# Key-bit rows inside the third score product of two periods, a new order of the first eight periods, and halved last products

## The chip, the cores and the metric

One core of one Trainium2 chip runs the whole program. The metric is the device time of one execution in microseconds (us). Engines are named as in the profile: PE (TensorE matmul), PEld (its weight load), DVE (VectorE), ACT (ScalarE), POOL (GpSimd), SP (SyncE, which issues all transfers here; its queue is SPq).

## What is computed

Bucketed attention over 2 batches, 8 heads, 768 positions and 64 channels, then two channel-mixing blocks. Only the attention concerns the change:

```python
q_bits = (np.einsum('bhsd,dk->bhsk', q, proj) > 0)      # 6 bits, a bucket number
k_bits = (np.einsum('bhsd,dk->bhsk', k, proj) > 0)
mask = q_bucket[:, :, :, None] == k_bucket[:, :, None, :]
scores = np.where(mask, scale * np.matmul(q, k.transpose(0, 1, 3, 2)), -1e9)
attn = exp(scores - max) / (sum + 1e-09)
x = attn @ v                      # then x = moe(x), x = moe2(x): 512 channels, 2048 hidden
```

moe2 ends in `x + relu(xn @ w_ch1) @ w_ch2`; its rows are the output of the kernel.

## The kernel before

Every product is made at reduced precision from a high and a low part (`hi`, `lo`), so one score tile is high x high, high x low and low x high. The equality of buckets is added to the scores by seven more rows of the contraction: six bits as large plus or minus values and one constant, so that a differing bucket sinks the score.

The attention runs in 48 periods (`NPER`) of two query tiles of 128 rows each. A head has three periods. A period p and tile i has: `S` or `D` (scores on PE, 128 x 772), `M` (row maximum, DVE), `E` (exponential, ACT), `R2` (reciprocal, DVE), `n` (normalising, POOL), `U` (12 transposes in three groups of four, PE), `H` and `L` (high and low part of the transposed weights, ACT and DVE), `PV` (12 products of 256 columns, PE), `O` and `X` (evacuation, ACT and DVE).

For heads 1 to 15 the operands are stacked by six transfers per head (`stack_dma`, lines 241 to 254; word `sk` in the order): `tq` x `tk` has 128 rows (high and low of q against high of k twice), `tq2` x `tk2` has 71 rows (high q against low k on rows 0 to 63, the bits on rows 64 to 70, put there by the two transfers of `stk_bits`, word `sb`). So a tile is four matmuls (`s_mm`, line 326). For head 0, the first three periods, nothing is stacked yet: `direct_mm` (line 497, word `D`) makes three products of two matmuls from the split tiles, with K = 64 rows in period 0 and K = 128 in periods 1 and 2, where `kz` is a copy of k with zeros in the lower 64 rows. `direct_bits` (line 512, word `Q`) then adds the bits by two matmuls of 7 rows.

What comes before the scores: `load0` and `raw_load` (`lr`) fetch q and k, `sh`/`sl` split them into high and low, `pb` splits the projection, `ac` (line 273) multiplies k and q by it for pair 0 (two matmuls for each half of k and q, x = 0, 1 for k and 2, 3 for q), `ay`, `ab`, `aw` turn the sign into bits on ACT, DVE and DVE or POOL; `bc`, `by`, `bb`, `bw` do this for pairs 1 to 3. `fk` writes two padding columns from the constants `cst_sb`.

Nothing schedules itself: each engine executes its instructions in the order in which the text `head` (line 684) names the steps, then the periodic `plan`, then the texts `tail`, `half1`, `trans`, and the rounds of the last block. One word is one step; a last number usually picks the engine (0: ACT or DVE, 1: POOL). All transfers go through SP's queue in the same order, and a transfer that waits for its data holds up those named behind it.

`warm(n)` (line 491) makes n transposes of the identity whose result nobody reads: 16 at the start, 17 in `head` between the bits of period 0 and `D.1.0`. At the end, `o_mm` (line 1172) makes the six matmuls of 512 columns of an output tile, `o_add` (line 1182) adds the residual and sends 128 rows of 2 KB out. The last round runs this for t = 0 to 5.

Of the kernel before, what the change touches and what calls it, by code (L numbers as in the profile page):

```python
# [9 lines left out]
F32 = mybir.dt.float32  # L10
F32R = mybir.dt.float32r
# [22 lines left out]
def attn_moe_kernel(  # L34
# [36 lines left out]
    def bank(tag, name):
        return psum.tile([128, 512], F32, tag=tag, name=name)
# [10 lines left out]
    M = const.tile([128, 4, 2, 2], F32, name="M")  # L83
# [181 lines left out]
    bits_t = {}  # L265
# [167 lines left out]
    def theta_steps(c, x, y):  # L433
# [19 lines left out]
    plan = (  # L453
# [15 lines left out]
    bk0 = wide(ap_, 64, "pn1", "bk0", 2)  # L469
# [20 lines left out]
    def warm(n):  # L490
        ps = bank("T0", "warm")
        for x in range(n):
            pe.transpose(ps[:, 0:128], ident, ident)  # L493

    def direct_mm(p, i):

        ps = psum.tile([128, 2, 512], F32, tag=f"S{i}", name=f"s{p}_{i}")
        s_ps[p, i] = ps
        r = slice((2 * p + i) * 128, (2 * p + i + 1) * 128)
        K, kk = (64, [hl["k", 0, y] for y in (0, 1)]) if p == 0 else (128, kz)  # L500
        for x, y in ((0, 0), (0, 1), (1, 0)):
            for hf in range(2):
                pe.matmul(  # L503
                    ps[:, hf, 0:HW], hl["q", 0, x][0:K, r],
                    kk[y][0:K, hf, :], start=(x + y == 0), stop=False,
                )

    def bits_q(r):
        hf, x = divmod(r.start, HALF)
        return bits_t[0][0:7, hf, x:x + 128]  # L510
# [72 lines left out]
    for i in range(8):  # L583
        c, x = divmod(i, 2)
# [74 lines left out]
    def bp_(x, e):  # L659
# [22 lines left out]
    )

    head = """
        sh.k.0.0.0 pb.0.0 pb.0.2 sl.k.0.0.0 pb.0.1 sh.k.0.1.0 sl.k.0.1.0 sh.q.0.0.0 sl.q.0.0.0 sh.q.0.1.0 ac.0
        sl.q.0.1.0 fk ac.1 ay.0 ay.1 kz.1.1 ac.2 ay.2 D.0.0 ab.0 lr.3.0 ab.1 ac.3 sh.k.1.2.0 D.0.1 ay.3 ab.2
        sh.q.1.2.0 aw.0.1 aw.1.1 pb.1.0 aw.2.0 kz.0.0 ab.3 Q.0.0 M.0.0 Q.0.1 warm.17 pb.1.2 E.0.0 lr.3.1 M.0.1
        sl.q.1.2.1 E.0.1 pb.1.1 D.1.0 sl.k.1.2.0 sh.k.3.2.0 Q.1.0 tb.0 lr.2.0 R2.0 lr.2.1 aw.3.0 M.1.0 n.0.1
        sk.1 sh.k.2.2.0 D.1.1 n.0.0 E.1.0 U.0.2 Q.1.1 U.0.0 sh.q.3.2.0 sl.k.2.2.0 sl.k.3.2.0 U.0.1 sl.q.3.2.1
        H.0.0 D.2.0 M.1.1 H.0.2 bc.0.1 L.0.2 L.0.0 Q.2.0 sh.q.2.2.0 E.1.1 M.2.0 by.0 tb.1 H.0.1 bc.1.0 D.2.1  # L690
        lv.0 bb.0 sl.q.2.2.1 L.0.1 by.1 sb.1 R2.1 Q.2.1 bw.0.1 n.1.0 E.2.0 bb.1 vh.0.0 lr.4.0 bc.3.1 M.2.1
        vh.0.1 S.3.0 lr.5.0 vl.0.0.0 bc.2.0 by.3 bw.1.1 E.2.1 U.1.0 by.2 M.3.0 S.3.1 bb.3 n.1.1 U.1.1 E.3.0
        vl.0.1.1 R2.2 bb.2 U.1.2 tb.2 bw.3.1 H.1.0 M.3.1 n.2.0 H.1.1 S.4.0 PV.0 H.1.2 E.3.1 L.1.0 L.1.1 lr.4.1
        M.4.0 tb.3 R2.3 sh.k.4.0.0 gl U.2.0 n.2.1 O.0 n.3.0 bw.2.1 L.1.2 X.0 S.4.1 sl.k.4.0.1 U.2.1 E.4.0 U.2.2
        H.2.0 M.4.1 H.2.1 sk.2 H.2.2 E.4.1 S.5.0 lv.1 sh.q.4.0.0 PV.1 lr.5.1 L.2.0 sb.2 L.2.1 M.5.0 L.2.2 R2.4
        O.1 tb.4 X.1 n.3.1 sh.k.4.1.1 E.5.0 U.3.0 S.5.1 U.3.2 U.3.1 n.4.1 H.3.0 H.3.2 H.3.1 S.6.0 M.5.1 sk.4
        n.4.0 L.3.0 vh.1.0 L.3.2 PV.2 E.5.1 L.3.1 sl.q.4.0.1 U.4.2 O.2 vh.1.1 M.6.0 sk.3 R2.5 X.2 vl.1.0.1
        U.4.0 sb.3 S.6.1 tb.5 H.4.0 sl.k.4.1.0 sb.4 U.4.1 H.4.2 M.6.1 n.5.0 E.6.0 H.4.1 L.4.0 E.6.1 PV.3 n.5.1
        S.7.0 U.5.0 sh.q.4.1.0 O.3 L.4.2 L.4.1 M.7.0 H.5.0 U.5.2 S.7.1 X.3 R2.6 tb.6 U.5.1 E.7.0 H.5.1 H.5.2
        M.7.1 PV.4 vl.1.1.1 L.5.0 sl.q.4.1.1 n.6.0 E.7.1 tb.7 O.4 L.5.1  # L700
    """

    for w in head.split():
# [284 lines left out]
    W1, W2 = {}, {}  # L988
# [135 lines left out]
    h_t, ps_t, sn_t, c_t, o_t = {}, {}, {}, {}, {}  # L1124
# [295 lines left out]
    zctx.close()  # L1420

# [49 lines left out]
```

## Time and profile before

| | us |
|---|---|
| three runs of the kernel before | 664.65, 665.45, 670.51 |
| their median | 665.45 |
| the profiled execution | 665.16 |
| its span, first to last instruction | 663.4 |
| PE busy in the span | 657.4 (99%) |
| DVE, ACT, POOL busy | 556.9, 416.7, 310.4 |

The profile is one execution. The span is 1.76 us shorter than the time of the same execution, which also holds what lies around it. Busy times of PE are modelled from pipelined matmuls; the distance between the starts of two matmuls of one row says what one costs in a stream. The chain of work is the path followed back from the last instruction; its pieces have a start, a length and a count.

### The profile page before, as it was taken

To read this page: it belongs to the slowest core of one execution; us is meant where nothing else is said; L and a number is where in the kernel's file an instruction comes from. 1 tells how busy PE (TensorE), PEld (TensorE's weight loads), DVE (VectorE), ACT (ScalarE), POOL (GpSimd) and SP (SyncE) were. 2 spreads that over 40 slices of the span, in tenths; PEclk is the share of its full clock that TensorE was granted. 3 is DMA by queue.
4 is the path that set the end of the run, shared out by engine and by line. 5 is a ranking of instruction groups with operands and counts; after the bars stand their busy time and mean duration, and the time that the engine had idled before them with its cause. 6 is when DMAs were issued, how large, how long until landed. Compare 5 with 4: busy or idle time off the path is not lost.

```text
span 663.4 us, 11202 instructions
## 1 busy us (share of the span) xinstructions
PE 657.4 (99%) x3769; PEld 591.7 (89%) x3769; DVE 556.9 (84%) x999; ACT 416.7 (63%) x864; POOL 310.4 (47%) x419
## 2 busy tenths in 40 slices
PE   9999999999999999999999999999999999999997
PEld 7999999999999888888888888989998999999996
DVE  6999998999999999999888889986767686867654
ACT  6899998999999886776435534553333433333321
POOL 5887887667787644233433133434150505051400
PEclk9999999999999999999999999999999999999999
DMA  8977544575530411222422122101112121311022
GB/s 247 241 172 171 142 106 114 126 165 124 132 91 1 160 54 57 81 77 98 144 81 64 48 96 68 60 1 64 64 65 75 53 96 34 105 53 33 0 80 111
DMA packets 32230, 62.24 MB, mean 94 GB/s; under 512 B 4466, under 2 KB 11460, under 8 KB 32173
## 3 DMA queue, kind: packets, MB, share of 16 engines
q1 hardware_dynamic: 32173, 61.53, 32.6%
q8 instruction: 30, 0.49, 0.3%
q14 instruction: 27, 0.22, 0.1%
HBM read 39.98 MB, written 3.15 MB: 65 GB/s over the span
## 4 chain that ended last, share of the span: by engine, by line
PE 96%; DVE 2%; DMA 1%; issue 0%; ACT 0%; SPq 0%; POOL 0%; POOLq 0%
PE o L1180 20%; PE acc L853 15%; PE o L405 10%; PE s L332 10%; PE t L380 9%; PE Z L1145 8%; PE a L895 5%; PE v L1145 5%; PE th L787 3%; PE zy L1145 2%; PE Y L1145 2%; PE bits L286 2%; PE s L503 1%; PE warm L493 1%; PE ut L880 1%; PE xt L964 1%
## 5 line engine op out<-in xcount | busy, mean ns | idle before, releaser
L1180 PE MATMUL o<-arena,hh 128*128 128x512 f32 x384 | 118.9, 391 | 0.0
L367 POOL TENSOR_SCALAR pn<-p,l,M 128x768 f32<-128x768 f32 x96 | 94.7, 986 | 38.6 <-DVE l L363 25.8
L340 DVE TENSOR_REDUCE M<-s 128x1 f32<-128x772 f32 x96 | 91.0, 949 | 3.6 <-PE s L515 2.2
L101 DVE TENSOR_TENSOR ptl<-t,pth 128x512 fp32r<-128x512 f32 x144 | 90.6, 680 | 1.5 <-ACT pth L389 1.3
L356 ACT ACTIVATE p<-s,M 128x772 f32<-128x772 f32 x96 | 87.6, 912 | 2.7 <-DVE M L340 2.2
L117 POOL TENSOR_SCALAR cs<-st 128x512 f32<-128x512 f32 (+2 forms) x68 | 44.7, 663 | 84.1 <-DVE cy L131 75.1
L1180 PEld LDWEIGHTS o<-arena,hh 128*128 128x128 f32 x384 | 71.5, 188 | 13.7
L389 ACT ACTIVATE pth<-t 128x512 fp32r<-128x512 f32 x144 | 81.1, 599 | 3.9 <-PE t L380 2.5
L332 PE MATMUL s<-tk,tq 128*128 128x386 f32 (+1 forms) x360 | 82.8, 351 | 0.0
L380 PE MATMUL t<-ident,pn 128*128 128x128 f32 x576 | 80.1, 273 | 0.0
L853 PE MATMUL acc<-arena,tokh 128*128 128x512 f32 x240 | 75.3, 395 | 0.0
L1180 PE MATMUL o<-arena,hl 128*128 128x512 f32 x192 | 75.2, 392 | 0.0
L380 PEld LDWEIGHTS t<-ident,pn 128*128 128x128 f32 x576 | 68.5, 141 | 5.7 <-POOL pn L367 0.6
L1153 ACT ACTIVATE sn<-Z 128x384 f32<-128x384 f32 x39 | 19.2, 492 | 67.2 <-PE Z L1145 67.2
L332 PEld LDWEIGHTS s<-tk,tq 128*128 128x128 f32 (+1 forms) x360 | 59.4, 190 | 0.1
L853 PEld LDWEIGHTS acc<-arena,tokh 128*128 128x128 f32 x240 | 44.0, 188 | 8.5
L1187 DVE TENSOR_TENSOR U<-o,U 128x512 f32<-128x512 f32 x48 | 32.9, 689 | 21.3 <-PE o L1180 20.5
L853 PE MATMUL acc<-arena,tokl 128*128 128x512 f32 x120 | 46.9, 391 | 0.0
L405 PE MATMUL o<-pth,vv 128*128 128x256 f32 x288 | 45.9, 295 | 0.1
L114 ACT ACTIVATE cy<-st 128x512 f32<-128x512 f32 (+2 forms) x72 | 39.6, 562 | 8.1 <-DVE tokl L101 2.5
L131 DVE SCALAR_TENSOR_TENSOR cy<-cy,cs 128x512 uint32<-128x512 uint32 (+2 forms) x72 | 41.4, 575 | 3.6
L125 DVE SCALAR_TENSOR_TENSOR cs<-st,cs 128x512 uint32<-128x512 uint32 (+2 forms) x76 | 44.0, 579 | 0.2
(257 smaller groups left out, 1482.8 us busy)
## 6 DMA issues: line engine op xcount, KB each, us to landing
st<-in_w_dram SPq DMA_DIRECT2D x36, 256.0 KB
st<-in_w_dram SPq DMA_DIRECT2D x14, 512.0 KB
tk<-hik SPq DMA_DIRECT2D x30, 193.0 KB
tq<-hiq SPq DMA_DIRECT2D x30, 192.0 KB
st<-in_wrT_dram SPq DMA_DIRECT2D x12, 384.0 KB
st<-in_wiT_dram SPq DMA_DIRECT2D x12, 384.0 KB
vs<-in_v_dram SPq DMA_DIRECT2D x8, 384.0 KB
tk<-lok SPq DMA_DIRECT2D x15, 193.0 KB
```

The costliest lines, as they stand in the source:

```text
L101: eng.tensor_tensor(out=o, in0=i, in1=f(hi), op=ALU.subtract)
L117: eng.tensor_scalar(out=s, in0=f(t)[:, :, 1], scalar1=0.0, scalar2=1.0, op0=ALU.mult, op1=ALU.mult)
L332: pe.matmul(ps[:, hf, 0:HW], lt[0:K, x * 128:(x + 1) * 128], rt[0:K, hf, :], start=(K == 128), stop=(K != 128),)
L340: vec.tensor_reduce(out=m_t[p][:, 0, i:i + 1], in_=s_ps[p, i][:, :, 0:HW], axis=AX.XY, op=ALU.max, negate=True)
L356: act.activation(pt, ps[:, :, 0:HW], AF.Exp, bias=m[:, 0, i:i + 1], accum_out=l_t[p][:, 0, i:i + 1])
L367: pool.tensor_scalar(out=pn.rearrange("p (h c) s -> p h (c s)", h=2), in0=p_t.pop((p, i))[:, :, 0:HALF], scalar1=l_t[p][:, 1, i:i + 1], sc ...
L380: pe.transpose(ps[:, w * 128:(w + 1) * 128], pn_t[p, i][:, c, :], ident)
L389: act.activation(ph, t_ps[p, u], AF.Copy)
L405: pe.matmul(ps, vv[:, c, e].rearrange("p a d -> p (a d)"), x[:, c::NI, :], start=(k == 0), stop=(k == 2 * NI - 1),)
L853: pe.matmul(acc, w[:, x, t * 128:(t + 1) * 128], z[:, x, y, :], start=(j == 0 and k == 0), stop=(j == NI - 1 and k == 5),)
L1145: pe.matmul(ps_t[r, b], W1[g][y][:, w, d, :], XB[s][x][:, z, d, :], start=(first == 1 and k == 0), stop=(k == 5), skip_group_check=True,)
L1180: pe.matmul(ps, lt[:, i * 128:(i + 1) * 128], W2[g][:, y, x, :], start=(k == 0), stop=(k == 5))
```

## The change

In periods 1 and 2 the third direct product becomes high q against low k over 71 rows: `tq2_0` (one more use of the ring `tq2`) takes high q by one transfer (`stack_q`, word `sq0`), and two transfers (`stack_b`, word `sb0`) put the bits of k on rows 64 to 70 of `kz[1]` and those of q on rows 64 to 70 of `tq2_0`. The steps `Q.1.0`, `Q.1.1`, `Q.2.0`, `Q.2.1` are gone; period 0 keeps its `Q`. The 16 transposes at the start become 38 products of a zeroed 128 x 128 part of `pb_lo` with itself, zeroed by DVE; the 17 later ones become 36. The order of the first eight periods is new. The last output tile is made in two halves of 256 columns in two banks, each added and sent by itself.

```diff
+    tq2_0 = bp.tile([128, S], F32R, tag="tq2", bufs=3, name="tq2z")
...
-        K, kk = (64, [hl["k", 0, y] for y in (0, 1)]) if p == 0 else (128, kz)
-        for x, y in ((0, 0), (0, 1), (1, 0)):
+        qh, ql = (hl["q", 0, y] for y in (0, 1))
+        kh, kl = [hl["k", 0, y] for y in (0, 1)] if p == 0 else kz
+        terms = ((qh, kh, 128), (ql, kh, 128), (tq2_0, kl, 71))
+        if p not in (1, 2):
+            K = 64 if p == 0 else 128
+            terms = ((qh, kh, K), (qh, kl, K), (ql, kh, K))
+        for x, (lt, rt, K) in enumerate(terms):
             for hf in range(2):
                 pe.matmul(
-                    ps[:, hf, 0:HW], hl["q", 0, x][0:K, r],
-                    kk[y][0:K, hf, :], start=(x + y == 0), stop=False,
+                    ps[:, hf, 0:HW], lt[0:K, r], rt[0:K, hf, :],
+                    start=(x == 0), stop=(x == 2 and p in (1, 2)),
                 )
+
+    def stack_q():
+        sp.dma_start(out=f(tq2_0[0:64]), in_=f(hl["q", 0, 0][0:64]))
+
+    def stack_b():
+        sp.dma_start(out=f(kz[1][64:71]), in_=f(bk0[0:7]))
+        sp.dma_start(out=f(halves(tq2_0[64:71])), in_=f(halves(bits_t[0][0:7])))
...
     sp.dma_start(out=pbr[:, 1:NP], in_=pb[:, 1:NP])
+    vec.memset(f(pb_lo[:, 1]), 0.0)
+    ps = bank("T0", "warm")[:, 0:128]
+    for x in range(38):
+        pe.matmul(ps, pb_lo[:, 1], pb_lo[:, 1], start=True, stop=True)
+    for n in (0, 2, 3):
+        vec.memset(f(pb_lo[:, n]), 0.0)
     make_identity(nc, ident)
     pool.memset(halfpi, math.pi / 2)
-    pool.memset(f(pb_lo), 0.0)
     for t in kz:
         pool.memset(f(t[64:128]), 0.0)
-    warm(16)
...
     head = """
-        sh.k.0.0.0 pb.0.0 pb.0.2 sl.k.0.0.0 pb.0.1 sh.k.0.1.0 sl.k.0.1.0 sh.q.0.0.0 sl.q.0.0.0 sh.q.0.1.0 ac.0
-        sl.q.0.1.0 fk ac.1 ay.0 ay.1 kz.1.1 ac.2 ay.2 D.0.0 ab.0 lr.3.0 ab.1 ac.3 sh.k.1.2.0 D.0.1 ay.3 ab.2
-        sh.q.1.2.0 aw.0.1 aw.1.1 pb.1.0 aw.2.0 kz.0.0 ab.3 Q.0.0 M.0.0 Q.0.1 warm.17 pb.1.2 E.0.0 lr.3.1 M.0.1
-        sl.q.1.2.1 E.0.1 pb.1.1 D.1.0 sl.k.1.2.0 sh.k.3.2.0 Q.1.0 tb.0 lr.2.0 R2.0 lr.2.1 aw.3.0 M.1.0 n.0.1
-        sk.1 sh.k.2.2.0 D.1.1 n.0.0 E.1.0 U.0.2 Q.1.1 U.0.0 sh.q.3.2.0 sl.k.2.2.0 sl.k.3.2.0 U.0.1 sl.q.3.2.1
-        H.0.0 D.2.0 M.1.1 H.0.2 bc.0.1 L.0.2 L.0.0 Q.2.0 sh.q.2.2.0 E.1.1 M.2.0 by.0 tb.1 H.0.1 bc.1.0 D.2.1
-        lv.0 bb.0 sl.q.2.2.1 L.0.1 by.1 sb.1 R2.1 Q.2.1 bw.0.1 n.1.0 E.2.0 bb.1 vh.0.0 lr.4.0 bc.3.1 M.2.1
...
+        sh.k.0.0.0 pb.0.0 sl.k.0.0.0 pb.0.2 pb.0.1 ac.0 sh.k.0.1.0 sh.q.0.0.0 sl.k.0.1.0 ac.1 sl.q.0.0.0
+        sh.q.0.1.0 sl.q.0.1.0 ay.0 ay.1 ac.2 ay.2 ac.3 fk ab.0 D.0.0 D.0.1 aw.0.1 ay.3 ab.1 aw.1.1 sq0 ab.2
+        aw.2.0 pb.1.0 pb.1.1 Q.0.0 Q.0.1 warm.36 ab.3 sh.k.1.2.0 lr.3.0 kz.1.1 aw.3.1 kz.0.1 M.0.0 lr.2.0 sb0
+        sh.q.1.2.0 M.0.1 lr.2.1 E.0.0 sl.q.1.2.0 sh.k.3.2.0 D.1.0 sl.k.1.2.0 sl.k.3.2.0 E.0.1 tb.0 sh.k.2.2.0
+        lr.3.1 pb.1.2 sk.1 sh.q.2.2.0 R2.0 sl.k.2.2.0 n.0.0 D.1.1 bc.0.1 sh.q.3.2.0 bc.1.0 U.0.0 lv.0 M.1.0
+        E.1.0 n.0.1 by.0 M.1.1 D.2.0 by.1 sl.q.2.2.0 bb.0 E.1.1 sb.1 tb.1 sl.q.3.2.1 U.0.1 bb.1 bw.0.1 H.0.0
+        H.0.1 U.0.2 H.0.2 M.2.0 L.0.0 D.2.1 E.2.0 vh.0.0 bc.2.1 lr.4.1 R2.1 vh.0.1 bw.1.1 L.0.2 n.1.0 by.2
+        M.2.1 E.2.1 vl.0.0.0 bc.3.0 L.0.1 tb.2 bb.2 S.3.0 n.1.1 M.3.0 vl.0.1.1 R2.2 U.1.0 by.3 sh.q.4.0.0 sk.2
...
-    def o_mm(r, t):
+    def o_mm(r, t, x0=None, tag=None):
...
-                pe.matmul(ps, lt[:, i * 128:(i + 1) * 128], W2[g][:, y, x, :], start=(k == 0), stop=(k == 5))
+                pe.matmul(ps, lt[:, i * 128:(i + 1) * 128], W2[g][:, y, x, n], start=(k == 0), stop=(k == 5))
...
-            sp.dma_start(out=out[c * 128:(c + 1) * 128, :], in_=u)
+            sp.dma_start(out=out[c * 128:(c + 1) * 128, cols(x0)], in_=u)
...
-    for t in range(1, 6):
+    for t in range(1, 5):
         run("o_mm.{r}.{t} o_add.{r}.{t}", r=r, t=t)
+    for x, tag in ((0, "O"), (1, "S0")):
+        run("o_mm.{r}.5.{x}.{tag} o_add.{r}.5.{x}", r=r, x=x, tag=tag)
```

## Rows read from the trace of the kernel before

**Rows 1.** The page, chain that ended last: shares of the span by engine.
```profile
PE 96%; DVE 2%; DMA 1%; issue 0%; ACT 0%; SPq 0%; POOL 0%; POOLq 0%
```

**Rows 2.** The chain in order of time, 0 to 60 us: start us, us, what.
```profile
1.34 3.69 PE warm L493 x16
...
5.07 2.29 PE bits L286 x6
7.36 1.27 PE s L503 x6
...
10.44 0.90 PE s L515 x4
11.34 2.01 PE warm L493 x17
13.35 1.11 PE s L503 x6
14.46 0.54 PE s L515 x2
15.00 1.26 PE s L503 x6
...
19.32 1.05 PE bits L286 x6
...
20.91 1.25 PE bits L286 x6
...
25.02 0.71 PE s L332 x4
...
29.54 1.45 PE o L405 x12
```

**Rows 3.** The timeline of PE: start us, us, line, operation, tile, shapes, count.
```profile
6.20 0.52 PE L286 MATMUL bits<-lok,pb_lo 128*128 128x384 f32 x1
6.52 0.52 PE L286 MATMUL bits<-hiq,pb_hi 128*128 128x384 f32 x1
```

**Rows 4.** The timeline of DVE; in brackets idle time before it and its releaser.
```profile
5.86 1.05 DVE L101 TENSOR_TENSOR loq<-raws,hiq 128x384 fp32r<-128x384 f32 x2
6.86 1.61 DVE L310 SCALAR_TENSOR_TENSOR bb<-bits,by 64x384 f32<-64x384 f32 x3
...
11.03 1.83 DVE L340 TENSOR_REDUCE M<-s 128x1 f32<-128x772 f32 x2 [0.73 <-PE s L515]
```

**Rows 5.** The timeline of POOL.
```profile
6.29 0.20 POOL L268 TENSOR_SCALAR bk<-cst_sb 64x4 fp32r<-64x4 f32 x1 [2.82 <-DMA cst_sb<-in_cst_dram]
6.55 1.05 POOL L98 TENSOR_SCALAR tk2z<-lok 64x772 fp32r<-64x772 f32 x1
...
7.63 1.30 POOL L523 TENSOR_SCALAR bk<-bb,cst_sb 64x384 fp32r<-64x384 f32 x2
```

**Rows 6.** The timeline of SP: the issue of transfers.
```profile
3.06 0.58 SPq L542 DMA_DIRECT2D cst_sb<-in_cst_dram  x1
...
8.26 0.66 SPq L248 DMA_DIRECT2D tq<-hiq  x1
...
13.54 1.00 SPq L174 DMA_DIRECT2D vs<-in_v_dram  x1
...
17.04 0.87 SPq L645 DMA_DIRECT2D tq<-bits  x1
```

**Rows 7.** Stretches of 5 us: length, busy by engine, granted clock, DMA share, GB/s.
```profile
5.00:10.00 5.00, 4.94 (x20) 3.95 (x20) 4.46 (x9) 4.32 (x9) 2.58 (x5) 1.00 0.97 319
...
20.00:25.00 5.00, 5.00 (x26) 4.00 (x25) 4.06 (x8) 4.01 (x9) 4.36 (x6) 1.00 1.08 299
...
35.00:40.00 5.00, 5.00 (x42) 4.91 (x41) 4.92 (x9) 4.93 (x13) 4.92 (x7) 1.00 0.98 208
```

**Rows 8.** The end of the same chain: start us, us, what.
```profile
651.31 8.22 PE o L1180 x36
...
659.55 0.69 DVE u L1187
```

**Rows 9.** Stretches at the end, columns as in rows 7.
```profile
661.00:661.50 0.50, 0.00 (x0) 0.00 (x0) 0.00 (x0) 0.00 (x0) 0.00 (x0) 1.00 0.77 303
661.50:662.00 0.50, 0.00 (x0) 0.00 (x0) 0.00 (x0) 0.00 (x0) 0.00 (x0) 1.00 0.58 221
```

More of the change, by code (lines that the diff above doesn't have):

```diff
@@ L679, in attn_moe_kernel @@
         vh=lambda n, x: v_hi(n, act, x), vl=lambda n, x, e: v_lo(n, ve[e], x),
-        D=direct_mm, Q=direct_bits, S=s_mm, M=s_max, E=s_exp, tb=s_lone, R2=s_recip,
+        sq0=stack_q, sb0=stack_b, D=direct_mm, Q=direct_bits, S=s_mm, M=s_max, E=s_exp, tb=s_lone, R2=s_recip,
         n=s_norm, U=p_transpose, H=p_hi, L=p_lo, PV=pv_mm, O=pv_evac_a, X=pv_evac_b,
@@ L690, in attn_moe_kernel @@
-        H.0.0 D.2.0 M.1.1 H.0.2 bc.0.1 L.0.2 L.0.0 Q.2.0 sh.q.2.2.0 E.1.1 M.2.0 by.0 tb.1 H.0.1 bc.1.0 D.2.1
-        lv.0 bb.0 sl.q.2.2.1 L.0.1 by.1 sb.1 R2.1 Q.2.1 bw.0.1 n.1.0 E.2.0 bb.1 vh.0.0 lr.4.0 bc.3.1 M.2.1
-        vh.0.1 S.3.0 lr.5.0 vl.0.0.0 bc.2.0 by.3 bw.1.1 E.2.1 U.1.0 by.2 M.3.0 S.3.1 bb.3 n.1.1 U.1.1 E.3.0
-        vl.0.1.1 R2.2 bb.2 U.1.2 tb.2 bw.3.1 H.1.0 M.3.1 n.2.0 H.1.1 S.4.0 PV.0 H.1.2 E.3.1 L.1.0 L.1.1 lr.4.1
-        M.4.0 tb.3 R2.3 sh.k.4.0.0 gl U.2.0 n.2.1 O.0 n.3.0 bw.2.1 L.1.2 X.0 S.4.1 sl.k.4.0.1 U.2.1 E.4.0 U.2.2
@@ L695, in attn_moe_kernel @@
[L695 to L699, printed above, removed]
@@ L700, in attn_moe_kernel @@
-        M.7.1 PV.4 vl.1.1.1 L.5.0 sl.q.4.1.1 n.6.0 E.7.1 tb.7 O.4 L.5.1
+        sh.k.0.0.0 pb.0.0 sl.k.0.0.0 pb.0.2 pb.0.1 ac.0 sh.k.0.1.0 sh.q.0.0.0 sl.k.0.1.0 ac.1 sl.q.0.0.0
+        sh.q.0.1.0 sl.q.0.1.0 ay.0 ay.1 ac.2 ay.2 ac.3 fk ab.0 D.0.0 D.0.1 aw.0.1 ay.3 ab.1 aw.1.1 sq0 ab.2
+        aw.2.0 pb.1.0 pb.1.1 Q.0.0 Q.0.1 warm.36 ab.3 sh.k.1.2.0 lr.3.0 kz.1.1 aw.3.1 kz.0.1 M.0.0 lr.2.0 sb0
+        sh.q.1.2.0 M.0.1 lr.2.1 E.0.0 sl.q.1.2.0 sh.k.3.2.0 D.1.0 sl.k.1.2.0 sl.k.3.2.0 E.0.1 tb.0 sh.k.2.2.0
@@ new lines, in attn_moe_kernel @@
+        lr.3.1 pb.1.2 sk.1 sh.q.2.2.0 R2.0 sl.k.2.2.0 n.0.0 D.1.1 bc.0.1 sh.q.3.2.0 bc.1.0 U.0.0 lv.0 M.1.0
+        E.1.0 n.0.1 by.0 M.1.1 D.2.0 by.1 sl.q.2.2.0 bb.0 E.1.1 sb.1 tb.1 sl.q.3.2.1 U.0.1 bb.1 bw.0.1 H.0.0
+        H.0.1 U.0.2 H.0.2 M.2.0 L.0.0 D.2.1 E.2.0 vh.0.0 bc.2.1 lr.4.1 R2.1 vh.0.1 bw.1.1 L.0.2 n.1.0 by.2
+        M.2.1 E.2.1 vl.0.0.0 bc.3.0 L.0.1 tb.2 bb.2 S.3.0 n.1.1 M.3.0 vl.0.1.1 R2.2 U.1.0 by.3 sh.q.4.0.0 sk.2
+        H.1.0 S.3.1 U.1.1 lv.1 PV.0 bw.2.1 M.3.1 bb.3 n.2.1 E.3.0 H.1.1 S.4.0 E.3.1 n.2.0 U.1.2 lr.5.0 L.1.0
@@ new lines, in attn_moe_kernel @@
+        U.2.0 S.4.1 sh.q.4.1.0 H.1.2 bw.3.1 L.1.1 M.4.0 lr.4.0 R2.3 tb.3 sl.q.4.0.1 L.1.2 O.0 E.4.0 X.0 M.4.1
+        H.2.0 n.3.1 U.2.1 U.2.2 H.2.1 vh.1.0 E.4.1 S.5.0 L.2.0 PV.1 H.2.2 O.1 n.3.0 U.3.0 L.2.1 sl.q.4.1.1
+        M.5.0 E.5.0 R2.4 sb.2 S.5.1 L.2.2 U.3.1 U.3.2 tb.4 X.1 H.3.0 S.6.0 PV.2 M.5.1 vl.1.0.1 H.3.1 n.4.0
+        L.3.0 H.3.2 L.3.1 M.6.0 E.5.1 R2.5 sh.k.4.0.1 lr.5.1 sh.k.4.1.0 n.4.1 O.2 sl.k.4.0.1 L.3.2 U.4.0 tb.5
+        E.6.0 S.6.1 sl.k.4.1.1 X.2 U.4.1 H.4.0 U.4.2 H.4.1 M.6.1 S.7.0 PV.3 H.4.2 L.4.0 E.6.1 L.4.1 vh.1.1
@@ L701, in attn_moe_kernel @@
+        n.5.0 M.7.0 U.5.0 S.7.1 n.5.1 tb.6 U.5.1 O.3 H.5.0 E.7.0 vl.1.1.1 L.4.2 R2.6 sk.3 X.3 U.5.2 H.5.1 n.6.0
+        M.7.1 PV.4 sk.4 H.5.2 sb.3 gl E.7.1 O.4 L.5.0 L.5.1 sb.4 tb.7
     """
@@ L1170, in h_lo, with cols @@
         vec.scalar_tensor_tensor(out=hlo, in0=c_t.pop((r, c)), scalar=0.0, in1=f(hh), op0=ALU.max, op1=ALU.subtract)
-    def o_mm(r, t):
+    def cols(x):
+        return slice(0, 512) if x is None else slice(256 * x, 256 * x + 256)
+    def o_mm(r, t, x0=None, tag=None):
         g, s = rounds[r]
         e, i = divmod(t, TB)
-        ps = o_t[r, t] = bank(("T0", "O")[t % 2], f"o{r}{t}")
+        n = cols(x0)
+        if tag == "S0":
+            ps = psum.tile([128, 2, 512], F32, tag=tag, name=f"o{r}{t}")[:, 0, n]
+        else:
+            ps = bank(tag or ("T0", "O")[t % 2], f"o{r}{t}")[:, n]
+        o_t[r, t] = ps
         k = 0
@@ L1179, in o_mm, with o_add @@
             for lt, y in ((hh, 0), (hh, 1), (hlo, 0)):
-                pe.matmul(ps, lt[:, i * 128:(i + 1) * 128], W2[g][:, y, x, :], start=(k == 0), stop=(k == 5))
+                pe.matmul(ps, lt[:, i * 128:(i + 1) * 128], W2[g][:, y, x, n], start=(k == 0), stop=(k == 5))
                 k += 1
-    def o_add(r, t):
+    def o_add(r, t, x0=None):
         g, s = rounds[r]
         c = ORD[6 * s + t]
-        u = U(c)
+        u = U(c)[:, cols(x0)]
         vec.tensor_tensor(out=u, in0=o_t.pop((r, t)), in1=u, op=ALU.add)
         if g == NG - 1:
-            sp.dma_start(out=out[c * 128:(c + 1) * 128, :], in_=u)
+            sp.dma_start(out=out[c * 128:(c + 1) * 128, cols(x0)], in_=u)
     ops.update(
```

## The prediction

> **What bounds the kernel now.** I read the page first, for the chain that ended last: PE holds 96% of it, nothing else over 2% [rows 1]. So the kernel is one queue of matmuls, and a change pays only by taking work out of that queue or by an earlier start or end. Next I read the chain in order of time through the first 60 us, which is where the order is new. From 1.34 us on each piece starts where the last one ends [rows 2]: PE waits for nobody, but two pieces are work that nobody reads, the 16 transposes of 3.69 us and the 17 of 2.01 us. They stand where PE would have waited for data, so waiting time is hidden in them. Third, the timeline of PE: at 6.20 and 6.52 us two matmuls of 384 columns start 0.32 us apart [rows 3], which is 1.2 columns per ns; six of them later take 1.05 us, 0.175 each [rows 2]. So the first 7 us run at the lower of the clock's two levels (1.2 and 2.4 GHz), though the granted clock reads 1.00 in that stretch [rows 7]. Last, the stretches: from 35 us on DVE and ACT are busy 4.92 and 4.93 of 5 us [rows 7], hardly less than PE. Whatever PE gains in the head, those two must gain as well.
>
> **The four bit products.** `Q.1` and `Q.2` were four pieces like that at 14.46, of 0.54 us [rows 2], though their two matmuls would take 0.37 by the 0.185 of a score matmul (six in 1.11). The rest is a change of the number of rows, and it is paid again by the piece behind: `D.1.1` takes 1.26 where `D.1.0` takes 1.11, and bits behind a `Q` take 1.25 where bits elsewhere take 1.05 [rows 2]. So a step costs 0.54 + 0.15 to 0.20, and four cost 2.8 to 3.0; I take 2.9. The third product with 71 rows is still two matmuls of 386 columns. Products of 128 and of 71 rows already alternate in `S`, whose four matmuls take 0.71 [rows 2], 0.18 each, so no such change is paid there. `D` keeps its price.
>
> **The dummies.** The later ones grow from 17 to 36: 2.01 / 17 is 0.118 each, so 36 take 4.26, 2.25 more. For the first ones, 38 products of 128 columns, no row shows a matmul below 256 columns that isn't a transpose. From below: by columns, a third of 0.32 is 0.107, 4.1 us in all. From above: no more than a 384-column product, 0.32, 12.2 us. Between them lies the transpose at the lower level, 3.69 / 16 = 0.231, 8.8 us. I take 0.107, because these are products of the same kind as those in [rows 3], whose time goes by columns, while a transpose moves another kind of data. They start behind one DVE memset instead of two POOL instructions, at about 1.0 (estimate), so they end at 5.1, as the old ones (5.03).
>
> **From there to `D.1.0`.** Eight bit matmuls now run in a row. At 0.32 they end at 7.65; at the higher level they would end at about 7.1, since the low part of the second half of q leaves DVE at 6.91 [rows 4]. I take 7.65. `D.0.0` takes 1.27 with its change of rows, `D.0.1` behind it 1.11: 10.0. `Q.0` takes 0.90: 10.9, and its inputs are there: DVE's three comparisons end at 8.47 [rows 4] and POOL makes two pieces of bits in 1.30 [rows 5]. The dummies end at 15.2. Before, `D.1.0` started at 13.35, so it starts 1.8 later. Its third product, 0.7 further on, needs `kz` and the three transfers. POOL does both copies now (1.05 each [rows 5]) and one more piece of bits (0.65): fourth comparison over at about 9.9, bits at 10.6, second copy at 11.7. `sb0` is issued at 10.6. A transfer of 1 KB behind earlier loads was issued at 3.06 and its reader ran at 6.29 [rows 5, 6], 3.2 us; that gives 13.8, and 2 us are left. So these edits cost nothing beside the dummies, which cover them; without that cover `D.1` would stand about 3 us behind `Q.0`.
>
> **The wait on SP.** `sb0` waits there for the bits, and `lr.2.1`, `lr.3.1`, six transfers of `sk.1`, `lv.0` and `sb.1` stand behind it. Before, `sk.1` was issued from 8.26, `lv.0` at 13.54 and the last bits of `sb.1` at 17.04 to 17.9 [rows 6]. Now `sk.1` begins at about 12.2 (`sb0` two issues of 0.4 to 0.9, two loads of 0.4), takes its 5.3 us, then `lv.0` 1.0 and `sb.1` 1.8: issued by 20.3, landed at 23.5 by the same 3.2 us. `S.3.0` needs it in its second product. After the gain it starts at 25.02 + 1.8 - 2.9 plus the 1.05 of a bits group moved ahead of it, 25.0, so about 1.9 us are left. The transfer engines are full here (share 1.08 [rows 7]), so this is the thinnest place.
>
> **Moves between engines.** DVE gives up one copy, one piece of bits and one low part of k, and takes two low parts of q; POOL the reverse; ACT does the same set. I put this at nothing: POOL has the room (2.58 of 5 us busy early [rows 7]), and DVE and ACT have about 0.5 to 1 us idle in each 5 us until 25 us. Zeroing `pb_lo` falls to DVE before its first data. Where DVE or ACT can't follow, up to 0.5 us of the gain is lost.
>
> **The end.** The last tile is 36 matmuls' last six, 0.228 each [rows 8]. Twelve of 256 columns take 1.45 [rows 2] against 1.37: 0.08 lost. The last addition shrinks from 0.69 [rows 8] to between 0.35 and 0.69; I take 0.45. The last transfer moves its 262 KB in about 0.8 us [rows 9]; half of it saves between nothing and 0.4, I take 0.25. Together 0.4 gained.
>
> **Sum.** 1.8 - 2.9 - 0.4 = -1.5. Against the profiled execution of 665.16 that is 663.7; the median stood 0.3 above it, so 664.0.
>
> **Rivals.** *The first dummies are dear* (slower than before). Per dummy x, `D.0.0` starts at 1.0 + 38x + 1.4, as eight bit matmuls at 0.175 follow. The gain is gone when it starts 1.5 later than the 7.65 forecast: x = 0.18. At the transpose's 0.231 it starts at 11.2: 3.5 lost, 667.5. At 0.32: 14.6, 671.0. For it speaks that every 128-column operation seen cost more than its columns; against it that the product is of the kind in [rows 3].
>
> *The clock falls under 36 transposes.* In the rows, 16 transposes over 3.69 us left the clock at the lower level, and it rose only behind 2.3 us of products (5.07 to 7.36); but 17 transposes over 2.01 us at the higher level did not lower it, for `D.1.0` ran at 0.185 behind them [rows 2]. If transposes don't hold the clock and 4.3 us are too long, some seven products run at 0.32 instead of 0.185 (1.0 us) and up to half of the dummies at 0.231 (2.0 us): 1 to 3 us, 665.0 to 667.0. The Trainium skill (TensorE: Matmul & The Clock Gate, Part 4, PE-mode transpose) says that transposes don't count as work for the clock. By that rule this rival would come true whenever the stretch is long enough; the sum would end at 665.0 to 667.0 by it and at 663.7 by the stretch of 17; the 3.69 us at the start agree with it, the 2.01 us neither show nor exclude it. Its chance goes by the rows, one stretch for each side and none of this length: 1 in 10.
>
> *SP's queue comes late.* If landing takes 2 us more than the 3.2 in the rows, the margins of 2 us are used up, and each further us is lost at `D.1` or `S.3`; with 2 us beyond, 666.0. Against it: before, 7 us lay between issue and use, so the row bounds nothing, but the queue has gaps to catch up in.
>
> *Nothing comes of it.* DVE and ACT, 98% busy from 35 us on, set the pace: PE arrives earlier and waits. 665.0 to 665.5.
>
> **Chances.** Forecast 0.60, with a range of its own of 662.8 to 665.0 (0.5 less for an earlier rise of the clock, 0.5 lost to DVE or ACT, the bounds of the end); dear dummies 0.12; clock 0.10; late queue 0.10; nothing 0.08. The range from 662.5 to 667.8 leaves out the upper half of the first rival, what is worse than 2 us of the queue, and a gain that I can't name: about 0.15. A measurement of this kernel can tell about 1% from no change. Faster by over 1% means under 658.8, and no row holds such a gain: the removed products and all later dummies are 5 us. Slower by over 1% means over 672.1, which needs two rivals at once. So 0.02, 0.94, 0.04.
>
> **What would show it.** Right: no `Q` pieces between `D.1.0` and `S.3.0`; first dummies over near 5.1 us with starts 0.107 apart; `D.1.0` near 15.2 without a wait; `PV.4`, PE's last step in the new order, some 1.1 us earlier than before; the last addition about 0.45. Wrong: dummies over 0.18 apart; 386-column matmuls 0.32 apart behind the 36; PE idle before `D.1.0`, its third product or `S.3.0`, released by a DMA; PE idle before `U`, `S` or `PV` behind ACT or DVE after 25 us.

## The result

The changed kernel takes 671.96 us (median of 11 runs, 669.94 to 674.87), the kernel before 664.84 (median of 11, with the three shown above among them). The ratio of the two is 1.0097, 95% interval 1.0081 to 1.0113: 6.4 us slower (the medians alone differ by 7.1). Forecast were 664.0 us and a range of 662.5 to 667.8.

The profiled execution took 670.53 us. The page of the changed kernel, span and busy times:

```profile
span 668.5 us, 11292 instructions
## 1 busy us (share of the span) xinstructions
PE 662.1 (99%) x3808; PEld 599.1 (90%) x3808; DVE 556.9 (83%) x1003; ACT 416.6 (62%) x864; POOL 310.6 (46%) x420
```

DVE, ACT and POOL do what they did; PE is busy longer although it lost eight bit matmuls, for it gained 41 dummies. The timeline of PE in the changed kernel (start us, us, line, operation, shapes, count, idle time before it and what ended that):

```profile
1.03 8.37 PE L561 MATMUL warm<-pb_lo 128*128 128x128 f32 x38 [1.03 <-DVE pb_lo L558]
9.46 0.69 PE L287 MATMUL bits<-hik,pb_hi 128*128 128x384 f32 x1
...
11.55 0.52 PE L287 MATMUL bits<-hiq,pb_hi 128*128 128x384 f32 x1
11.87 0.52 PE L287 MATMUL bits<-loq,pb_lo 128*128 128x384 f32 x1
12.32 0.91 PE L509 MATMUL s<-hik,hiq 64*128 64x386 f32 x2
13.07 0.51 PE L509 MATMUL s<-lok,hiq 64*128 64x386 f32 x2
13.42 0.52 PE L509 MATMUL s<-hik,loq 64*128 64x386 f32 x2
...
15.84 4.15 PE L494 MATMUL warm<-ident 128*128 128x128 f32 x36
19.74 0.61 PE L509 MATMUL s<-tkz,hiq 128*128 128x386 f32 x2
...
26.10 0.62 PE L509 MATMUL s<-tkz,hiq 128*128 128x386 f32 x2 [1.41 <-ACT p L357]
...
33.46 0.98 PE L333 MATMUL s<-tk,tq 128*128 128x386 f32 x4 [0.62 <-ACT p L357]
...
663.89 0.40 PE L1205 MATMUL o<-arena,hh 128*128 128x256 f32 x2
```

Three things are to be seen. The 38 zero products take 8.4 us, 0.22 each on average, and the bits start at 9.46 instead of 5.07 [rows 2]. The bits are still 0.32 us apart, and the direct products come to 0.36 for two, the higher level of the clock, only from 13.07 on; before, that was so from `D.0.0` at about 7.4. And PE, which waited for nobody, now waits 1.41 us before `D.2.0` (26.10) and 0.62 us before `S.3.1` (33.46), both times for exponentials on ACT.

In the same view of the kernel before, `D.1.0` starts at 13.14 and the last tile at 657.99:

```profile
13.14 0.62 PE L503 MATMUL s<-tkz,hiq 128*128 128x386 f32 x2
...
657.99 0.62 PE L1180 MATMUL o<-arena,hh 128*128 128x512 f32 x2
```

With those the two profiled executions divide so:

| stretch | before | after | change | forecast |
|---|---|---|---|---|
| start of the span to `D.1.0` | 13.14 | 19.74 | +6.6 | +1.8 |
| `D.1.0` to the last tile's first matmul | 644.85 | 644.15 | -0.7 | -2.9 |
| from there to the end of the span | 5.38 | 4.60 | -0.8 | -0.4 |
| span | 663.37 | 668.49 | +5.1 | -1.5 |

Why ACT was late is told by its own timeline and by SP's, both of the changed kernel:

```profile
22.84 0.85 ACT L211 ACTIVATE hiq<-raw 128x768 fp32r<-128x768 f32 x1 [2.59 <-DMA raw<-in_qT_dram]
24.32 0.84 ACT L211 ACTIVATE hiq<-raws 128x768 fp32r<-128x768 f32 x1 [0.63 <-DMA raws<-in_qT_dram]
25.07 0.89 ACT L357 ACTIVATE p<-s,M 128x772 f32<-128x772 f32 x1
```

```profile
7.51 0.50 SPq L166 DMA_DIRECT2D raw<-in_kT_dram  x1
13.02 0.87 SPq L518 DMA_DIRECT2D tk2z<-bk  x1
15.56 0.86 SPq L519 DMA_DIRECT2D tq2z<-bits  x1
16.47 0.43 SPq L166 DMA_DIRECT2D raw<-in_qT_dram  x1
16.95 0.41 SPq L166 DMA_DIRECT2D raws<-in_qT_dram  x1
```

SP issued nothing from 8.0 to 13.0 us: `sb0` waited for the bits, and the two loads of q behind it left at 16.47 and 16.95. ACT waited for them with `E.1.0` (25.07) queued behind, and `D.2.0` needs the bank that `E.1.0` frees. Meanwhile the transfer engines had little to do. Stretches of 5 us of the changed kernel, columns as in [rows 7]:

```profile
10.00:15.00 5.00, 5.00 (x21) 4.31 (x19) 3.54 (x6) 3.68 (x7) 2.27 (x5) 1.00 0.34 119
15.00:20.00 5.00, 5.00 (x42) 4.75 (x42) 4.41 (x6) 3.35 (x7) 2.39 (x8) 1.00 0.50 151
```

Their share is 0.34 and 0.50 where the neighbouring stretches of the kernel before have 0.97 and 1.08 [rows 7].

### The profile page after: what moved, and what is told of

Same layout as the page of the kernel before. It is cut to its first block, busy times and chain, and to the rows that moved or that the text cites. A ratio compares the mean times of both kernels' runs of the same rounds, so it can differ in the third digit from the quotient of the medians.

```text
span 668.5 us, 11292 instructions
## 1 busy us (share of the span) xinstructions
PE 662.1 (99%) x3808; PEld 599.1 (90%) x3808; DVE 556.9 (83%) x1003; ACT 416.6 (62%) x864; POOL 310.6 (46%) x420
## 4 chain that ended last, share of the span: by engine, by line
PE 96%; DMA 2%; ACT 0%; DVE 0%; SPq 0%; POOL 0%; issue 0%
PE o L1205 20%; PE acc L870 15%; PE o L406 10%; PE s L333 10%; PE t L381 9%; PE Z L1162 8%; PE a L912 5%; PE th L804 5%; PE v L1162 5%; PE zy L1162 2%; PE Y L1162 2%; PE bits L287 1%; PE warm L561 1%; DMA tq<-hiq 1%; DMA raws<-in_qT_dram 1%; PE ut L897 1%
## 5 line engine op out<-in xcount | busy, mean ns | idle before, releaser
L1205 PE MATMUL o<-arena,hh 128*128 128x512 f32 (+1 forms) x388 | 119.2, 388 | 0.0
L1205 PE MATMUL o<-arena,hl 128*128 128x512 f32 (+1 forms) x194 | 75.5, 389 | 0.0
L1212 DVE TENSOR_TENSOR U<-o,U 128x512 f32<-128x512 f32 x48 | 32.9, 689 | 21.2 <-PE o L1205 20.5
```

Of the source, the lines that this page charges most:

```text
L1205: pe.matmul(ps, lt[:, i * 128:(i + 1) * 128], W2[g][:, y, x, n], start=(k == 0), stop=(k == 5))
```

## Experiments

Times are given as ratios to the kernel before, measured beside it on the same chip; 0.001 is 0.66 us. "The way behind" is the span less the start of `D.1.0`: 650.2 for the kernel before, 648.8 for the changed one.

### Half of the first dummies

```diff
-    for x in range(38):
+    for x in range(19):
```

> The changed kernel with 19 instead of 38 of the zero products at the start. Theory (the first dummies are dear): each costs 0.22 us, so 19 end at about 5.2 us instead of 9.4, the bit products follow at once and end near 7.7, and D.1.0 starts near 15.5 instead of 19.7; 4.2 us come back, and the kernel stands 1 to 2 us above the kernel before. Rival (the head is bound by loads and bits, and the dummies only fill a wait): D.1.0 moves less than 1.5 us and the time stays 4 us or more above.

1.0035 (1.0021 to 1.0050), 4.1 us less than the changed kernel. The timeline of PE in this run:

```profile
1.03 4.32 PE L561 MATMUL warm<-pb_lo 128*128 128x128 f32 x19 [1.03 <-DVE pb_lo L558]
...
8.58 1.01 PE L509 MATMUL s<-hik,hiq 64*128 64x386 f32 x2
9.39 0.84 PE L509 MATMUL s<-lok,hiq 64*128 64x386 f32 x2
10.04 0.84 PE L509 MATMUL s<-hik,loq 64*128 64x386 f32 x2
...
14.32 5.55 PE L494 MATMUL warm<-ident 128*128 128x128 f32 x36
19.62 0.61 PE L509 MATMUL s<-tkz,hiq 128*128 128x386 f32 x2
```

The price of a dummy is settled: 19 take half of what 38 take, and the time falls by 4.1 us where 4.2 were expected. But the profiled execution doesn't show it at `D.1.0`. There the clock stayed at its lower level through all direct products (0.64 for two) and the bits, and rose only within the 36 transposes. My expectation had the start right and left out the clock. In that execution the loads had time to land: PE waited for none in the head, and the way behind is 646.8, 3.4 us less than before: 2.6 up to the last tile (661.83 - 19.62 = 642.2 against 644.85) and 0.8 in the end. The 2.6 are what the forecast's step for the removed bit products, 2.9, comes to together with the new order.

### The same dummies with 256 columns

```diff
+    vec.memset(f(kz[1][:, 0, 0:256]), 0.0)
-    ps = bank("T0", "warm")[:, 0:128]
-    for x in range(38):
-        pe.matmul(ps, pb_lo[:, 1], pb_lo[:, 1], start=True, stop=True)
+    ps = bank("T0", "warm")[:, 0:256]
+    for x in range(19):
+        pe.matmul(ps, pb_lo[:, 1], kz[1][:, 0, 0:256], start=True, stop=True)
...
```

> As the run with 19 zero products, but each with 256 columns of zeros instead of 128. Theory (a product has a floor that 128 columns don't reach, the weight load): 256 columns cost about the same 0.22 to 0.24 us as 128, and the dummies end within 0.4 us of the other run's; the time is the same within 0.5 us. Rival (two cycles for each column of such a product): 0.43 us each, 8.2 us in all, ending near 9.4, and the time is that of the changed kernel. Apart from both: if denser dummies lift the clock, the bit products stand less than 0.32 us apart before 7 us.

1.0036 (1.0024 to 1.0048). The timeline of PE:

```profile
1.31 4.05 PE L562 MATMUL warm<-tk2z,pb_lo 128*128 128x256 f32 x19 [1.31 <-DVE tk2z L559]
5.42 0.44 PE L287 MATMUL bits<-hik,pb_hi 128*128 128x384 f32 x1
5.70 0.34 PE L287 MATMUL bits<-lok,pb_lo 128*128 128x384 f32 x1
5.87 0.33 PE L287 MATMUL bits<-hik,pb_hi 128*128 128x384 f32 x1
...
14.40 0.60 PE L509 MATMUL s<-tkz,hiq 128*128 128x386 f32 x2
...
27.99 0.98 PE L333 MATMUL s<-tk,tq 128*128 128x386 f32 x4 [1.52 <-ACT p L357]
```

Nineteen products of 256 columns take from 1.31 to 5.42 us, 0.216 each: twice the columns for the same time. The last few already run at the higher level, but before them the single starts in the trace stand 0.213 us apart, as those of the 128-column products in the changed kernel do. So 128 columns cost what 256 cost. That there is a floor is shown; that it is the weight load is only argued. Behind these dummies the bits stand 0.17 us apart from the second one on: the clock is up before 5.7 us, and `D.1.0` starts at 14.40. Now that PE is early, the late loads cost more: the way behind is 650.3, 3.5 us longer than in the run before, 2.6 of it lost by `S.3.1`, and the time is no better than that of the run before.

### Loads ahead of the bits

```diff
-... M.0.0 lr.2.0 sb0
-        sh.q.1.2.0 M.0.1 lr.2.1 E.0.0 ... sh.k.2.2.0
-        lr.3.1 pb.1.2 sk.1 ...
+... M.0.0 lr.2.0 lr.2.1 lr.3.1 sb0
+        sh.q.1.2.0 M.0.1 E.0.0 ... sh.k.2.2.0
+        pb.1.2 sk.1 ...
```

> The changed kernel with the two loads of q (lr.2.1, lr.3.1) put on SP's queue ahead of the two transfers of bits (sb0) instead of behind; nothing else differs, all 38 dummies are there. Theory (sb0 waits on SP for the bits and holds the loads up): the waits of ACT for these loads (2.6 and 0.6 us) are gone, E.1.0 is over before PE comes to D.2.0, and PE's waits of 1.4 us there and of 0.6 us behind it shrink to under 0.5 together; 2 to 3 us less than the changed kernel. Rival (the transfer engines are full, order does not matter, other transfers come late instead): under 0.7 us less.

1.0095 (1.0074 to 1.0115): no gain that can be measured. In the profiled execution the waits went as expected: ACT splits q at 22.09 and 22.82 without waiting, and PE waits for nothing but 0.6 us for POOL and 0.4 us later on. But there the clock rose only within the 36 transposes, `D.1.0` started at 23.31, and then the loads would have been in time anyway. By itself this run decides nothing; the same edit with the clock up, in the next section, does.

### Both: 256 columns and loads first

> Both at once: 19 zero products of 256 columns at the start, and the two loads of q ahead of the transfers of bits. Theory (removing the four bit products is worth 2.9 us once nothing is late): D.1.0 starts near 14.4 us as in the run with 256 columns, PE's waits of 0.4 and 1.5 us behind it are gone, the way from D.1.0 to the end is about 647 us as with the 19 products of 128 columns (646.8) instead of 650.3; the span is near 661.5 and the time 0.2 to 0.4% below the kernel before. Rival (the transfer engines are full, and what is taken from one wait comes back in another): no more than 0.1% below the run with 256 columns alone, that is above the kernel before.

0.9983 (0.9968 to 0.9998), 3.5 us less than with 256 columns alone. PE's waits for ACT are gone. The timeline of PE:

```profile
6.28 0.52 PE L287 MATMUL bits<-lok,pb_lo 128*128 128x384 f32 x1
6.60 0.52 PE L287 MATMUL bits<-hik,pb_hi 128*128 128x384 f32 x1
...
15.16 0.60 PE L509 MATMUL s<-tkz,hiq 128*128 128x386 f32 x2
...
16.66 0.60 PE L509 MATMUL s<-tk2z,tq2z 71*128 71x386 f32 x2 [0.54 <-DMA tq2z<-bits]
```

With the loads ahead it is the bits that come late, 0.54 us in `D.1.0`. The way behind is 647.7. The same dummies left the clock low for longer this time, with bits 0.32 us apart behind them, so `D.1.0` starts at 15.16 instead of 14.40, and 0.17% is just short of the 0.2 to 0.4 expected. So SP's queue is what cost the changed kernel its waits, and the theory of this pair holds; the rival, that full transfer engines make order indifferent, falls.

### The bit products back

```diff
-        if p not in (1, 2):
+        if True:
...
-... sq0 ... sb0 ... D.1.0 ... D.1.1 ... D.2.0 ... D.2.1 ...
+... D.1.0 Q.1.0 ... D.1.1 Q.1.1 ... D.2.0 Q.2.0 ... D.2.1 Q.2.1 ...
```

> The changed kernel with the bits of periods 1 and 2 as separate products again: three direct products and two bit matmuls for each of four tiles, without the three transfers sq0 and sb0. Theory (the stacking takes 2.9 us off PE and gives 3.1 back in waits that sb0 causes): the time is that of the changed kernel within 0.7 us, with four pieces of bits back and no wait of PE before D.2.0. Rival (the waits come from the new order itself, not from sb0): 2 to 3 us slower than the changed kernel.

1.0123 (1.0109 to 1.0138): 1.7 us slower than the changed kernel, between what theory and rival said. The waits before `D.2.0` are gone, as expected of `sb0`: ACT splits the two loads of q at 19.90 and 20.63 without waiting. The way behind is 649.9. So the stacking was worth more than its waits cost, by 1.1 us in the two profiled executions (648.8); by the runs the two intervals just overlap. From `D.1.0` to the last tile it is 645.1 us (666.27 - 21.16), 2.9 more than with half of the dummies, which has no wait in the head either: that is the price of the four bit products in one order. And it is 0.3 more than in the kernel before (644.85), which has them too: that is what the new order costs. Stretches of this run, columns as in [rows 7]:

```profile
12.60:16.00 3.40, 3.40 (x19) 2.90 (x19) 2.79 (x5) 2.04 (x4) 2.36 (x5) 0.98 1.06 266
16.00:18.00 2.00, 2.00 (x11) 2.00 (x10) 2.00 (x4) 1.60 (x3) 1.18 (x5) 0.50 1.05 227
18.00:20.00 2.00, 2.00 (x15) 2.00 (x14) 2.00 (x5) 2.00 (x6) 0.20 (x3) 0.69 1.20 240
20.00:22.00 2.00, 2.00 (x18) 2.00 (x17) 0.74 (x1) 1.47 (x3) 1.78 (x3) 1.00 1.03 252
```

The granted clock fell to 0.50, the lower level, at about 16 us, while PE did nothing but transposes (15.6 to 21.2), and came back during them. Ahead of the fall stood the products of 64 and of 7 rows. So a clock that falls under the 36 transposes, the forecast's rival, does occur, here in one execution. But it fell 0.3 us after they began, not for the length of the stretch, and it came back while they went on.

### The old start

```diff
-    vec.memset(f(pb_lo[:, 1]), 0.0)
-    ps = bank("T0", "warm")[:, 0:128]
-    for x in range(38):
-        pe.matmul(ps, pb_lo[:, 1], pb_lo[:, 1], start=True, stop=True)
-    for n in (0, 2, 3):
-        vec.memset(f(pb_lo[:, n]), 0.0)
+    pool.memset(f(pb_lo), 0.0)
+    warm(16)
```

> The changed kernel with the old start: 16 transposes of the identity instead of 38 zero products, all else as changed. Theory (the 38 products are what puts D.1.0 late, by their own length and by what they leave of the clock): the dummies end at 5.0 us, the clock rises near 7.3 us as in the kernel before, D.1.0 starts at 14.9 to 15.3; the waits behind it stay, so 0.2 to 0.5% above the kernel before. Rival (the clock's rise depends on what follows, eight bit products and then products of 64 and 7 rows): the clock stays low to the dummies behind Q, D.1.0 starts near 19 and the time is 0.6% or more above.

1.0012 (0.9996 to 1.0027). The timeline of PE:

```profile
5.41 0.34 PE L287 MATMUL bits<-lok,pb_lo 128*128 128x384 f32 x1
5.58 0.33 PE L287 MATMUL bits<-hik,pb_hi 128*128 128x384 f32 x1
```

`D.1.0` starts at 14.33, earlier than expected, since the clock is up from 5.4 us on, with bits 0.17 apart, and not from 7.3. The waits of 1.3 and 0.3 us for ACT stay. Of the 6.4 us that the change lost, 5.6 go with the start alone.

### The same kernel twice more

> The changed kernel once more, unchanged, for a second profiled execution; its runs lie between 669.9 and 674.9 us. Theory (the spread is the moment at which the clock rises): in another execution the rise falls elsewhere between 10 and 22 us, D.1.0 moves with it by half of the shift and more (18.5 to 23 us), and the span follows by the same amount, less what PE then waits less behind it. Rival (the spread comes from transfers): the rise and D.1.0 stay within 0.3 us of 12.9 and 19.7, and waits behind D.1.0 differ.

> A third profiled execution of the changed kernel, for the same question, with the same expectations: by the first theory D.1.0 and the span move together with the rise of the clock, by the rival only the waits behind D.1.0 differ.

669.05 and 673.60 us. The timeline of PE, first of the one:

```profile
13.13 0.61 PE L509 MATMUL s<-lok,hiq 64*128 64x386 f32 x2
13.59 0.51 PE L509 MATMUL s<-hik,loq 64*128 64x386 f32 x2
...
19.90 0.60 PE L509 MATMUL s<-tkz,hiq 128*128 128x386 f32 x2
...
25.18 0.62 PE L509 MATMUL s<-tkz,hiq 128*128 128x386 f32 x2 [0.33 <-ACT p L357]
```

and of the other:

```profile
12.32 1.01 PE L509 MATMUL s<-hik,hiq 64*128 64x386 f32 x2
13.13 0.84 PE L509 MATMUL s<-lok,hiq 64*128 64x386 f32 x2
...
15.70 0.84 PE L509 MATMUL s<-hik,loq 64*128 64x386 f32 x2
...
18.05 5.72 PE L494 MATMUL warm<-ident 128*128 128x128 f32 x36
23.53 0.60 PE L509 MATMUL s<-tkz,hiq 128*128 128x386 f32 x2
```

Up to 12.3 us the three executions of the kernel are alike to 0.01 us. Then the clock rises at about 13 us in two, and in the third only within the transposes: `D.1.0` is 3.6 to 3.8 us later. That is the first theory. But the rival holds beside it: the wait before `D.2.0` is 1.41, 0.33 and none, where the first two have the same `D.1.0` to 0.2 us, as the loads issued at 16.47 and 16.95 in both landed sooner in one. The spans are 668.5, 667.1 and 670.9. The eleven runs of the result fall into two groups, with spans of 668.0 to 669.0 us in five and of 670.2 to 672.8 in six. That a late rise makes the upper group is likely by these three, and not shown.

### Fewer transposes behind `Q`

```diff
-        ... Q.0.0 Q.0.1 warm.36 ab.3 ...
+        ... Q.0.0 Q.0.1 warm.17 ab.3 ...
```

> The changed kernel with 17 instead of 36 transposes behind Q. Forecast's step: the dummies cover the landing of the bits; without 19 of them (2.1 us at the higher level, 4.4 at the lower) D.1.0 starts that much earlier and its third product waits for the bits (issued at 15.6, landing by 18.8). Theory: D.1.0 is earlier by 2 us, but E.1.0 stands behind the two late loads of q on ACT, so D.2.0 starts where it did (26.1) and no more than 0.5 us is gained; where the clock stays low, the gain is larger, up to 2 us. Rival (the dummies are pure loss): 2 us or more in each run, 0.3% and more below the changed kernel.

1.0051 (1.0036 to 1.0066), 3 us less than the changed kernel: I had said 0.5, or up to 2 with a low clock, and the rival, that these dummies are pure loss, 2 or more; the rival came nearer. `D.1.0` starts at 17.86 and its third product at 18.64 without a wait, so the dummies covered nothing there. `D.2.0` starts at 24.65, with a wait of 1.24 us for ACT: 1.4 us earlier than at 26.10, since the second load of q was split from 22.87 instead of 24.32. The rest of the 3 us isn't explained by this profiled execution (670.28, the slowest of its five): its span is 668.5, as that of the changed kernel. That 17 transposes lose less than 36 wherever the clock is low fits its narrower runs (668.2 to 670.3) and is argued, not shown.

### The halved last tile alone, on the kernel before

> The kernel before with one part of the change alone: the last output tile in two halves of 256 columns. Forecast's step: 0.08 us lost in matmuls, 0.25 us gained in the addition, 0.25 in the transfer, 0.4 us in all (0.06%), with a bound of 0.1 to 0.7. Rival: nothing, the end is set by the landing of the last transfer whatever its size.

0.9979 (0.9964 to 0.9995). From the last tile's first matmul to the end of the span it takes 4.81 us (657.13 to 661.94) instead of 5.38; in the changed kernel it is 4.60. In the timeline of DVE of the changed kernel the last addition is the forecast's 0.45:

```profile
665.52 0.42 DVE L1212 TENSOR_TENSOR u<-o,u 128x256 f32<-128x256 f32 x1 [0.29 <-PE o L1205]
```

So the part is worth 0.6 to 0.8 us, and the forecast's 0.4 was low. The ratio says 1.4 us, with an interval of 0.3 to 2.4, and can't tell more; in the profiled execution PE also came to the last tile 0.86 us earlier, by nothing that the edit touches.

### Two repairs further

Both start from the run with 256 columns and loads first. In the first, the second part of the projection goes behind the fourth comparison:

```diff
-        aw.2.0 pb.1.0 pb.1.1 Q.0.0 ...
+        aw.2.0 Q.0.0 ...
-        sh.q.1.2.0 M.0.1 E.0.0 ...
+        sh.q.1.2.0 pb.1.0 M.0.1 pb.1.1 E.0.0 ...
```

> As the run before it, and the second part of the projection (pb.1.0 on ACT, pb.1.1 on DVE) goes behind the fourth comparison (ab.3) and the split of pair 1 instead of ahead of them. In the run with 256 columns ACT waited 2.05 us for that part's load with the splits and the last bits queued behind. Theory: the last piece of bits leaves POOL near 9.8 us instead of 11.9, sb0 and the six transfers of sk.1 are issued 1.5 to 2 us earlier; D.1.0 stays where the 36 dummies put it, so the time is the same or up to 0.15% lower where a late transfer still holds S.3. Rival (the bits set D.1.0): D.1.0 itself moves forward by a microsecond or more.

0.9977 (0.9961 to 0.9993). The last transfer of bits is issued at 10.55 instead of 13.82, and `D.1.0`'s third product still waits 0.36 us: issued early, the bits stand behind four loads on the queue. (That the bits are what is late is argued from this product's operands; the profile ends the wait with a transfer of `tk` issued behind them.) The span's start and `D.1.0` (14.62) are as the dummies put them. Then one of the two loads back behind the bits:

> The run with 256-column zeros, loads first and bits first, with one of the two loads (lr.3.1) back behind the bits, so that 393 KB less stand ahead of them on the queue. Theory: the bits land about 1.2 us earlier, the wait of 0.4 us in D.1.0 is gone, nothing else moves: 0.2 to 0.35% below the kernel before. Rival: the load is late for ACT instead, and D.2.0 waits: no better than 0.2%.

0.9981 (0.9970 to 0.9992). The wait in `D.1.0` is gone, as expected, and 0.19 us before `S.3.1` has come; the time is short of the 0.2% or more expected. A stretch, columns as in [rows 7]:

```profile
10.00:15.00 5.00, 5.00 (x42) 4.75 (x43) 4.51 (x6) 3.98 (x9) 1.84 (x8) 1.00 1.00 318
```

The transfer engines are full again, and the three intervals of the repaired kernels lie on one another. These versions lie 0.2% below the kernel before, but so does the last tile alone: that the repaired head adds anything to it is not shown.

## Why the prediction was wrong

*The bound* was read rightly: PE is the chain, and each us that it starts late or waits in the head is in the end of the span.

*The bit products*: 2.9 forecast; 2.9 measured between the two runs of one order, 2.6 with what the order costs. Right.

*The first dummies*: this is the step that failed. I bounded a product of 128 columns by 0.107, 0.231 and 0.32 and took the lowest, because time had gone by columns in [rows 3]. Those rows show it for 384 columns and no fewer. The product costs 0.22, as much as one of 256, and close to the transpose's 0.231, the only row with 128 columns. So the dummies ended at 9.4 us and not at 5.1. The rival *the first dummies are dear* had this price, and gave 667.5 for it; it was the case that came true, and I gave it 0.12. The term is 4.3 us.

*From there to `D.1.0`*: I had the eight bit matmuls at the lower level and all behind them at the higher. In two of three profiled executions of the changed kernel the rise comes at about 13 us, within `D.0.0`, instead of 7.4; in the third, and with half of the dummies, the direct products and the bits were slow too. The prediction took the rise in the kernel before, behind 2.3 us of products, as given. It was one execution: behind the same 16 transposes the clock was up by 5.4 us in the runs with the old start and with the last tile alone. The rival on the clock looked at the 36 transposes alone. It had nothing for a start whose dummies leave the clock low for longer.

*The wait on SP*: I listed what stands behind `sb0`, took the thinnest margin at `S.3.0`, and missed the load of q that ACT needs for a split queued ahead of `E.1.0`, and the bank that `E.1.0` frees for `D.2.0`. I followed the held transfers to their first readers, not from the readers to what stands behind them on their engine. It cost 1.9 us in the profiled execution (644.15 against 642.2), 0.3 in another. The late dummies are not its cause: with 256 columns, where the bits started near the forecast, the two transfers of `sb0` left at 8.79 and 11.95, about the 10.6 forecast, and PE waited 0.37 and 1.52 us for ACT. The rival *SP's queue comes late* had the queue, with 0.10, but looked for the loss in what `D.1` and `S.3` read themselves, and not in the loads behind the bits.

*Moves between engines* cost next to nothing: with the bit products back, `D.1.0` to the last tile is 0.3 us longer than before, the order included. *The end*: 0.4 forecast, 0.6 to 0.8 measured.

The sum with the measured terms: 1.8 + 4.3 for the start, 0.5 more for what is between the dummies and `D.1.0`, -2.6 for the bits, +1.9 of waits, -0.8 at the end: 5.1, the change of the span. The 0.5 is what is left over, not a measured term. Two rivals at once, which I had called for to be over 1%, is what happened, and it came to just under that. What the runs have beyond this (6.4 by the ratio) is as much as the moment of the clock's rise moves from one execution to the next; the two groups of runs fit a rise that comes late in about half of them, which is not shown.

## What to carry to other kernels

A price taken from rows of one size holds down to that size; below it, take the nearest row of the new size, even if it is of another kind. A transfer that must wait for fresh data goes behind the loads on its queue, and each load held up is followed to its reader and then to what is queued behind that reader. Dummies that fill the start should be judged by what they leave of the clock as well as by their length.

## What the runs showed of the hardware

At the lower clock the single starts of zero products stand 0.213 us apart in the trace, with 128 columns (38 and 19 in a row) as with 256 (19 in a row, up to the rise); the 384 columns of the bits take 0.32.

The moment at which the clock rises differs between executions that begin alike. With 38 of the narrow products, over 8.4 us, it rose at 12.3 to 13.3 us in four of six profiled executions, and in two only within the 36 transposes. With 19 of the wide ones, zeros as well, it was up at 4.7 to 7.2 us in four, not always by their end. With the 16 transposes it was up at 5.1 to 7.3 us in three. So not the data but the form of the dummies differed.

In the run with 19 narrow ones the clock then stayed low through 12 direct products of 64 rows and four of 7, from 8.6 to 14.3 us, and rose within the transposes. The Trainium skill (TensorE: Matmul & The Clock Gate, Part 4, PE-mode transpose) says that transposes don't count as work for the clock. Three profiled executions here contradict it: with half of the dummies, with the loads ahead of the bits and in the third execution of the changed kernel, the clock rose 2.8 to 3.3 us after the 36 transposes began, while PE did transposes only. In the run with the bit products back it fell and rose again during them. What exactly decides is open.
